# One layout for the four leading expert blocks: seven products first, then their second products, with the Sinkhorn steps at listed points

## The chip, the cores and the metric

The kernel runs on one core of a Trainium2 chip. The metric is the device time of one execution in microseconds (us). Engines are named as in the profile: PE (TensorE), DVE (VectorE), ACT (ScalarE), POOL (GpSimd), SP (the queue that issues DMAs). Each engine runs its instructions in program order, and waits on semaphores where an operand or a buffer is not ready.

## What is computed

Three stages follow one another: a sparse attention (2 batches, 8 heads, 768 tokens, 64 features), a mixture of 8 experts over 1536 tokens of 512 features, and a two-layer network with a rational activation. The change lies in the middle stage:

```python
logits = x @ w_gate                      # 1536 x 8
P = np.exp(logits - logits.max())
for _ in range(8):                       # Sinkhorn steps
    P /= P.sum(1, keepdims=True) + 1e-09
    P /= P.sum(0, keepdims=True) + 1e-09
    P *= N / E
for e in range(E):
    h = np.maximum(x @ w1[e], 0.0)       # 512 -> 1024
    out += P[:, e:e + 1] * (h @ w2[e])   # 1024 -> 512
```

## The kernel before, in words

All matrix products are made of three fp32r matmuls, from operands split into a high and a low part (`hh`, `hl` of a hidden tile, `w2h`, `w2l` of a weight). The order on each engine is the order in which the code is written.

An expert is two units of 512 hidden columns. Unit 0 is done in the plain way, partly under the attention. Units 1 to 15 are cut into halves: sub-units v = 0 to 29, each with 256 hidden columns in two chunks c. Each sub-unit has two blocks, j = 0 and 1, of 768 tokens. A block is written (v, j) here.

- A block makes its hidden layer by a Strassen-like scheme of **seven products** (`product`, six matmuls of 384 columns each) into three PSUM accumulators X, Y and Z (one bank each). DVE and ACT combine them in `s1`, `s2`, `s3`; `hidden(c, half, src)` then makes the relu `hh` on ACT and the rest `hl` on DVE. There are four hidden tiles: two chunks, two halves of the tokens. The last, `hidden(1, 0, X)`, reads the seventh product's X.
- Then come six **second products** (`g2w`, six matmuls of 512 columns each, tile `p_v`): three groups of 128 tokens for each half. DVE adds each to the output sums `accs`. Their PSUM tiles come from a pool of three banks (`psm`); for the later blocks a ring uses two further banks (`psb`) as well.
- In the **later blocks** (v >= VG = 2) the seven products stand in a row (order 0, 2, 1, 4, 3, 6, 5), then three second products held over from the block before (`held`, its half 1), then three of the block's own half 0.
- In the **four leading blocks** (v = 0, 1) the products are in the order 0 to 6, and after each one `step` calls `tick`: it runs a job if one is due, and one second product from the queue `g2q`. So products and second products alternate, and second products run a block after their hidden tiles. The seventh product is added into Y; `hidden(0, 1, s2)` waits in `late` for the next block.
- The **jobs** are the Sinkhorn steps. `sk_max_b` and `sk_max_c` spread the maximum (two small matmuls `mxt`, `mxb`); `sk_first` then normalizes the rows; each `sk_step` is a matmul with ones (`csp`) and nine small DVE operations (four for the columns, L972 to L975, five for the rows, L963 to L967; the last step has only the four). `point` counts calls of `tick`; a job runs at the first point at or after its due number.
- **Weights**: POOL splits the quarters of w1 and their sums (`w_sums`, `w_op`) and w2 (`w2_op`) for the next sub-unit. For v = 0, `w2_op(0, 0)` is written before block (0, 0), into the pool `cv`, and `w2_op(0, 1)` after its seventh product. The conversion of the last stage's weights (`cv_load`, `cv_round`, `cv_join`, `cv_add`, `cv_high`, `cv_low`, `cv_store`) runs beside the blocks from v = 2 on, with a first part in (1, 1).

Three second products of unit 0 are left when block (0, 0) starts; they have twelve matmuls each.

Of the kernel before, what the change touches and what calls it, by code (L numbers as in the profile page):

```python
# [22 lines left out]
def kernel(  # L23
# [1087 lines left out]
    jobs += [(4, sk_max_b), (7, sk_first)]  # L1111
    jobs += [(9 + 2 * i + (i > 1), lambda i=i: sk_step(i == 7)) for i in range(8)]
# [43 lines left out]
    VG = 2  # L1156
    LATER = [0, 2, 1, 4, 3, 6, 5]

    def turn(v, i):
        return LATER[i] if v >= VG else i  # L1160

    def w_op(v, i):
        i = turn(v, i)
# [6 lines left out]
    def w2_op(v, c):  # L1170
        st = sg["v", v, 2]
        pool, tag = (vpool, "cv") if v == c == 0 else (w2pool[1], "w2")
        hi = pool.tile([P, DM], F32R, tag=tag, name=f"w2h_v{v}_{c}")
        lo = pool.tile([P, DM], F32R, tag=tag, name=f"w2l_v{v}_{c}")
        split(hi, lo, st[:, c, :])
        wt["v", v, c] = (hi, lo)

    def sub_weights(v, j, i):

        n = v + 1  # L1180
        if j == 0:
# [25 lines left out]
    late = []  # L1207
# [3 lines left out]
    def step(v):  # L1211
        tick()

    def block(v, j):
# [12 lines left out]
        def product(i, ps, get, start):  # L1227
# [7 lines left out]
            sub_weights(v, j, turn(v, i))  # L1235
# [12 lines left out]

        if v >= VG:
            k = 2 * (v - VG) + j  # L1250
            product(0, X, xs(0, o1), True)
            nc.scalar.copy(s1, X)  # L1252
            if k == 0:
                while late:
                    late.pop()()
                for _ in range(n // P):
                    g2q.pop(0)[1]()
                held[:] = [f for _, f in g2q]
                g2q.clear()
            cv_add(k)  # L1260
            product(2, Z, xs(1, o1), True)
            nc.vector.tensor_add(s1, s1, Z)
            cv_join(k + 1)
# [4 lines left out]
            nc.vector.tensor_add(s2, s2, Y)
            cv_high(k)
            product(3, X, tt(1), False)  # L1270
            nc.scalar.copy(s3, X)
            nc.vector.tensor_add(s3, s3, Y)
            product(6, Z, xs(1, o2), True)
            hidden(1, 1, s3)
# [184 lines left out]
```

## Time and profile before

| what | value |
|---|---|
| median of 3 runs | 1351.94 us (1351.87 to 1351.96) |
| profiled execution | 1352.21 us, span of the trace 1350.5 us |
| PE busy | 1342.1 us (99%) |
| DVE busy | 1052.9 us (78%) |
| POOL busy | 804.3 us (60%) |
| ACT busy | 510.9 us (38%) |

Matmuls are pipelined: the listed duration of one overlaps the next, so PE's pace is read from the starts of its matmuls, not from their durations or from the busy share. DVE's instructions overlap their neighbours by about 0.1 us in the same way.

### The profile page before, as it was taken

The numbers are of one execution on the slowest core, as the hardware profiler recorded it, in microseconds if no ns is written. First come the engines' busy times: TensorE is split into PE (matmuls) and PEld (weight loads), VectorE is DVE, ScalarE is ACT, GpSimd is POOL, SyncE is SP. The second block draws the span as 40 slices with busy tenths as digits, with TensorE's granted clock in tenths as the row PEclk, the third lists the DMA queues.
The fourth block names the chain that finished last, engine by engine and source line by source line (L and its number), as shares of the span: only waits on it lengthen the run. The fifth ranks groups of instructions, "written<-read, shape, count | busy, mean of one in ns | idle before, by whom it ended". The sixth has DMA issues, their size and how long they took to land.

```text
span 1350.5 us, 20263 instructions
## 1 busy us (share of the span) xinstructions
PE 1342.1 (99%) x7343; PEld 1186.0 (88%) x7343; DVE 1052.9 (78%) x1956; ACT 510.9 (38%) x1136; POOL 804.3 (60%) x983
## 2 busy tenths in 40 slices
PE   8999999999999999999999999999999999999999
PEld 6888898999999999999999999999999888888887
DVE  7775588777777777777787777777777689988885
ACT  6874313222222222222222222222222379866662
POOL 7625747777776777776777767777777012222221
PEclk9999999999999999999999999999999999999999
DMA  9730112222222222222222222222222411312102
GB/s 262 169 85 1 51 46 63 89 70 79 67 73 68 67 77 67 83 66 87 69 77 72 67 74 68 76 69 77 75 80 62 146 57 47 94 33 94 32 16 78
DMA packets 122004, 102.40 MB, mean 76 GB/s; under 512 B 36272, under 2 KB 102960, under 8 KB 121904
## 3 DMA queue, kind: packets, MB, share of 16 engines
q1 hardware_dynamic: 121904, 101.10, 25.7%
q8 instruction: 58, 0.95, 0.3%
q14 instruction: 42, 0.34, 0.1%
HBM read 81.15 MB, written 19.92 MB: 75 GB/s over the span
## 4 chain that ended last, share of the span: by engine, by line
PE 97%; DVE 1%; DMA 1%; ACT 0%; SPq 0%; issue 0%; POOL 0%; DVEq 0%; ACTq 0%
PE p_v L185 12%; PE p_v L184 12%; PE p_v L186 12%; PE p L184 8%; PE p L186 8%; PE p L185 8%; PE X L1234 6%; PE X L1232 6%; PE X L1233 6%; PE Z L1233 3%; PE Z L1234 3%; PE Z L1232 3%; PE Y L1234 2%; PE Y L1233 2%; PE Y L1232 2%; PE xo L678 1%
## 5 line engine op out<-in xcount | busy, mean ns | idle before, releaser
L1347 DVE SCALAR_TENSOR_TENSOR accs<-p_v,Pt,accs 128x512 f32<-128x512 f32 x336 | 244.4, 746 | 85.9 <-PE p_v L186 85.2
L184 PE MATMUL p_v<-w2h_v,hh_v 128*128 128x512 f32 x720 | 282.2, 392 | 0.1
L186 PE MATMUL p_v<-w2h_v,hl_v 128*128 128x512 f32 x720 | 281.9, 392 | 0.0
L185 PE MATMUL p_v<-w2l_v,hh_v 128*128 128x512 f32 x720 | 281.7, 391 | 0.0
L1241 DVE SCALAR_TENSOR_TENSOR hl_v<-s,hh_v 128x384 fp32r<-128x384 f32 x180 | 137.4, 763 | 76.0 <-ACT hh_v L1240 74.6
L234 POOL TENSOR_TENSOR hl<-ta,hh 128x512 fp32r<-128x512 f32 x48 | 62.5, 1302 | 204.4 <-ACT hh L233 150.0
L1252 ACT COPY s<-X 128x384 f32<-128x384 f32 x56 | 27.0, 482 | 406.6 <-PE X L1234 406.6
L1041 POOL TENSOR_SCALAR ce<-ce 128x296 uint32<-128x296 uint32 (+1 forms) x56 | 67.1, 1199 | 176.7 <-DVE ce L1032 176.7
L186 PEld LDWEIGHTS p_v<-w2h_v,hl_v 128*128 128x128 f32 x720 | 135.2, 188 | 28.3
L184 PEld LDWEIGHTS p_v<-w2h_v,hh_v 128*128 128x128 f32 x720 | 135.4, 188 | 26.3 <-DVE accs L1342 0.5
L185 PEld LDWEIGHTS p_v<-w2l_v,hh_v 128*128 128x128 f32 x720 | 135.3, 188 | 25.9
L1240 ACT ACTIVATE hh_v<-s 128x384 fp32r<-128x384 f32 x180 | 94.9, 527 | 126.8 <-DVE s L1275 68.6
L110 POOL TENSOR_TENSOR wS<-S,wS 128x256 fp32r<-128x256 f32 x120 | 100.2, 835 | 14.4 <-ACT wS L107 4.7
L184 PE MATMUL p<-xh,w1h 128*128 128x512 f32 (+2 forms) x272 | 100.8, 371 | 0.0
L186 PE MATMUL p<-xh,w1l 128*128 128x512 f32 (+2 forms) x272 | 99.1, 364 | 0.0
L185 PE MATMUL p<-xl,w1h 128*128 128x512 f32 (+2 forms) x272 | 99.1, 364 | 0.0
L184 PE MATMUL p<-w2h,hh 128*128 128x512 f32 (+1 forms) x240 | 94.0, 392 | 0.0
L186 PE MATMUL p<-w2h,hl 128*128 128x512 f32 (+1 forms) x240 | 93.3, 389 | 0.0
L185 PE MATMUL p<-w2l,hh 128*128 128x512 f32 (+1 forms) x240 | 93.2, 388 | 0.0
L110 POOL TENSOR_TENSOR w2l_v<-sb,w2h_v 128x512 fp32r<-128x512 f32 x60 | 82.9, 1382 | 5.0
L1234 PE MATMUL X<-th,wS 128*128 128x384 f32 x240 | 80.3, 335 | 0.0
L1232 PE MATMUL X<-th,wS 128*128 128x384 f32 x240 | 80.3, 335 | 0.0
(249 smaller groups left out, 3309.1 us busy)
## 6 DMA issues: line engine op xcount, KB each, us to landing
sa<-in_moe_w_dram SPq DMA_DIRECT2D x30, 512.0 KB, 3.4
sb<-in_moe_w_dram SPq DMA_DIRECT2D x30, 512.0 KB, 4.3
cv<-in_moe_w_in_dram SPq DMA_DIRECT2D x24, 296.0 KB, 2.9
w1h<-f_in SPq DMA_DIRECT2D x16, 256.0 KB, 2.8
w1l<-f_in SPq DMA_DIRECT2D x16, 256.0 KB, 3.2
w2h<-f_out SPq DMA_DIRECT2D x16, 256.0 KB, 4.9
w2l<-f_out SPq DMA_DIRECT2D x16, 256.0 KB, 5.1
vx<-in_v_dram SPq DMA_DIRECT2D x20, 192.0 KB, 4.2
```

The costliest lines, as they stand in the source:

```text
L110: nc.gpsimd.tensor_sub(lo, src, hi.bitcast(F32))
L184: nc.tensor.matmul(ps, lhsT=sh, rhs=mh, start=(i == 0), stop=False)
L185: nc.tensor.matmul(ps, lhsT=sh, rhs=ml, start=False, stop=False)
L186: nc.tensor.matmul(ps, lhsT=sl, rhs=mh, start=False, stop=(i == n_k - 1))
L234: nc.gpsimd.tensor_sub(hl[:, :n], ta, hh[:, :n].bitcast(F32))
L1041: nc.gpsimd.tensor_scalar(out=e, in0=e, scalar1=896, scalar2=0, op0=ALU.subtract, op1=ALU.max)
L1232: nc.tensor.matmul(ps, lhsT=w[:, 0, t], rhs=mh, start=start and t == 0, stop=False, **go)
L1233: nc.tensor.matmul(ps, lhsT=w[:, 0, t], rhs=ml, start=False, stop=False, **go)
L1234: nc.tensor.matmul(ps, lhsT=w[:, 1, t], rhs=mh, start=False, stop=t == 1, **go)
L1240: nc.scalar.activation(hh, src, AF.Relu)
L1241: nc.vector.scalar_tensor_tensor(out=hl, in0=src, scalar=0.0, in1=hh.bitcast(F32), op0=ALU.max, op1=ALU.subtract)
L1347: nc.vector.scalar_tensor_tensor(out=a, in0=ps, scalar=Pt[:, g, e:e + 1], in1=a, op0=ALU.mult, op1=ALU.add)
```

## The change

The branch for the leading blocks goes. Every block has the layout of the later ones: the seven products in the order 0, 2, 1, 4, 3, 6, 5, the seventh in a bank of its own (Z) with one more DVE addition, then the held second products, then the block's own three. In (0, 0) nothing is held yet; unit 0's three second products stand behind its first product. In the leading blocks a job can run behind the first product, behind the fourth one written (product 4), and behind each second product; the due numbers are given for these points. `w2_op(0, 0)` and `w2_op(0, 1)` are both written behind the second product of (0, 0), in the pool of the other w2 tiles. The conversion's first part follows the later blocks' places. Where the ring of PSUM banks starts (v = 2) is unchanged.

```diff
-    jobs += [(4, sk_max_b), (7, sk_first)]
-    jobs += [(9 + 2 * i + (i > 1), lambda i=i: sk_step(i == 7)) for i in range(8)]
+    jobs += [(1, sk_max_b), (2, sk_first)]
+    jobs += [(due, lambda i=i: sk_step(i == 7)) for i, due in enumerate((4, 7, 9, 12, 15, 18, 21, 23))]
...
             if v == 0:
-                if i == 2:
+                if i == 1:
+                    w2_op(0, 0)
+                    w2_op(0, 1)
+                    dma_sub(1, 2)
+                elif i == 2:
                     w_sums(1)
                 elif 2 < i < 6:
                     w_op(1, i - 3)
-                elif i == 6:
-                    w2_op(0, 1)
-                    dma_sub(1, 2)
...
+    def turn_on():
+        point[0] += 1
+        run_job()
...
+        k = 2 * (v - VC) + j
         product(0, X, xs(0, o1), True)
         nc.scalar.copy(s1, X)
-        while late:
-            late.pop()()
-        step(v)
-        product(1, X, tt(0), False)
-        nc.scalar.copy(s2, X)
-        step(v)
+        if v == j == 0:
+            for _, f in g2q:
+                f()
+            g2q.clear()
+        if v < VC:
+            turn_on()
+        if k >= 0:
+            cv_add(k)
         product(2, Z, xs(1, o1), True)
         nc.vector.tensor_add(s1, s1, Z)
+        if k + 1 >= 0:
+            cv_join(k + 1)
+        product(1, X, tt(0), False)
+        nc.scalar.copy(s2, X)
         hidden(0, 0, s1)
...
+        product(4, Y, xs(0, o2), True)
+        nc.vector.tensor_add(s2, s2, Y)
+        if k >= 0:
+            cv_high(k)
+        else:
+            turn_on()
         product(3, X, tt(1), False)
         nc.scalar.copy(s3, X)
-        step(v)
-        product(4, Y, xs(0, o2), True)
         nc.vector.tensor_add(s3, s3, Y)
+        product(6, Z, xs(1, o2), True)
         hidden(1, 1, s3)
-        step(v)
+        nc.vector.tensor_add(s2, s2, Z)
+        if k >= 0:
+            cv_low(k)
         product(5, X, tt(2), False)
+        hidden(0, 1, s2)
         hidden(1, 0, X)
...
+        for i, f in enumerate(held + seconds_of(0)):
+            f()
+            if i == 0 and k >= 0:
+                cv_store(k)
+            elif i == max(2, len(held)) and k + 2 >= 0:
+                cv_round(k + 2)
+            turn_on()
+        held[:] = seconds_of(1)
```

Two places show the new order. The first is PE at the end of block (0, 0); the product from `wA` into X is the one that `hidden(1, 0, X)` reads. Before:

```order
L1234 MATMUL X_0_2163<-th_1804,wA_0_2155 128x384
L184 MATMUL p_0_8_2268<-w2h_0_746,hh_768_0_1988 128x512
L185 MATMUL p_0_8_2268<-w2l_0_747,hh_768_0_1988 128x512
L186 MATMUL p_0_8_2268<-w2h_0_746,hl_768_0_1989 128x512
L184 MATMUL p_0_8_2268<-w2h_1_750,hh_768_1_2087 128x512
L185 MATMUL p_0_8_2268<-w2l_1_751,hh_768_1_2087 128x512
```

Now:

```order
L1230 MATMUL X_0_2159<-th_1804,wA_0_2154 128x384
L184 MATMUL p_v_0_2310<-w2h_v_0_2224,hh_v_0_00_2247 128x512
L185 MATMUL p_v_0_2310<-w2l_v_0_2225,hh_v_0_00_2247 128x512
L186 MATMUL p_v_0_2310<-w2h_v_0_2224,hl_v_0_00_2248 128x512
L184 MATMUL p_v_0_2310<-w2h_v_1_2228,hh_v_0_10_2306 128x512
L185 MATMUL p_v_0_2310<-w2l_v_1_2229,hh_v_0_10_2306 128x512
L186 MATMUL p_v_0_2310<-w2h_v_1_2228,hl_v_0_10_2307 128x512
```

Behind that product stood a second product of unit 0, whose hidden tiles were old; now the block's own first second product stands there, and its fourth matmul reads `hh_v_0_10`, made from that same X.

The second place is DVE in block (0, 1): a Sinkhorn step between the sums of the products. Before:

```order
L1241 SCALAR_TENSOR_TENSOR hl_v_1_10_2432<-X_1_2295,hh_v_1_10_2431 128x384
L972 TENSOR_SCALAR cr<-csp 128x8
L973 RECIPROCAL cr<-cr 128x8
L974 TENSOR_SCALAR cr<-cr 128x8
L975 TENSOR_TENSOR Pt<-Pt,cr 128x96
L963 TENSOR_REDUCE rs<-Pt 128x12
L964 TENSOR_SCALAR rs<-rs 128x12
L965 RECIPROCAL rr<-rs 128x12
L966 TENSOR_TENSOR Pt<-Pt,rr 128x96
L967 TENSOR_REDUCE cs<-Pt 128x8
L1342 TENSOR_TENSOR accs<-accs,p_v_4_2446 128x512
L1318 TENSOR_TENSOR s_0_1_2299<-s_0_1_2299,Y_1_2296 128x384
```

Now:

```order
L1264 TENSOR_TENSOR s_0_1_2349<-s_0_1_2349,Y_1_2346 128x384
L972 TENSOR_SCALAR cr<-csp 128x8
L973 RECIPROCAL cr<-cr 128x8
L974 TENSOR_SCALAR cr<-cr 128x8
L975 TENSOR_TENSOR Pt<-Pt,cr 128x96
L963 TENSOR_REDUCE rs<-Pt 128x12
L964 TENSOR_SCALAR rs<-rs 128x12
L965 RECIPROCAL rr<-rs 128x12
L966 TENSOR_TENSOR Pt<-Pt,rr 128x96
L967 TENSOR_REDUCE cs<-Pt 128x8
L1271 TENSOR_TENSOR s_0_1_2350<-s_0_1_2350,Y_1_2346 128x384
L1237 SCALAR_TENSOR_TENSOR hl_v_1_11_2433<-s_0_1_2350,hh_v_1_11_2432 128x384
```

The step stood behind the block's `hl_v_1_10`; now it stands ahead of three of the block's four `hl` tiles, and the additions of the second products stand behind all four.

## Rows read from the trace of the kernel before

**Rows 1.** The page: PE's busy time, its granted clock, the chain that ended last.

```profile
PE 1342.1 (99%) x7343; PEld 1186.0 (88%) x7343; DVE 1052.9 (78%) x1956; ACT 510.9 (38%) x1136; POOL 804.3 (60%) x983
...
PEclk9999999999999999999999999999999999999999
...
PE 97%; DVE 1%; DMA 1%; ACT 0%; SPq 0%; issue 0%; POOL 0%; DVEq 0%; ACTq 0%
```

**Rows 2.** Waits of PE, whole span, first of seven: total us, times, longest.

```profile
PE spin L540 <- POOL ident masks.py:199: 1.4, 1, 1.4
```

**Rows 3.** Timeline of PE, first matmul of blocks (0,0) to (3,0): start us, duration us.

```profile
137.84 0.33 PE L1232 MATMUL X<-xh,wA 128*128 128x384 f32 x1
...
153.60 0.33 PE L1232 MATMUL X<-xh,wA 128*128 128x384 f32 x1
...
170.27 0.33 PE L1232 MATMUL X<-xh,wA 128*128 128x384 f32 x1
...
186.67 0.33 PE L1232 MATMUL X<-xh,wA 128*128 128x384 f32 x1
...
203.03 0.34 PE L1232 MATMUL X<-xh,wA 128*128 128x384 f32 x1
...
223.09 0.33 PE L1232 MATMUL X<-xh,wA 128*128 128x384 f32 x1
...
238.60 0.33 PE L1232 MATMUL X<-xh,wA 128*128 128x384 f32 x1
```

**Rows 4.** Timeline of PE around the matmul of one Sinkhorn step.

```profile
161.10 0.28 PE L971 MATMUL csp<-cs,ones 128*128 128x8 f32 x2
161.23 0.48 PE L184 MATMUL p_v<-w2h_v,hh_v 128*128 128x512 f32 x1
161.55 0.39 PE L185 MATMUL p_v<-w2l_v,hh_v 128*128 128x512 f32 x1
```

**Rows 5.** Timeline of all engines at the seventh product's end, block (2,1).

```profile
229.03 0.56 DVE L1272 TENSOR_TENSOR s<-s,Y 128x384 f32<-128x384 f32 x1 [0.56 <-ACT s L1271]
...
230.40 0.39 PE L184 MATMUL p_v<-w2h_v,hh_v 128*128 128x512 f32 x1
...
231.72 0.47 ACT L1240 ACTIVATE hh_v<-X 128x384 fp32r<-128x384 f32 x1
...
232.33 0.55 DVE L1241 SCALAR_TENSOR_TENSOR hl_v<-X,hh_v 128x384 fp32r<-128x384 f32 x1
...
232.84 0.75 DVE L1347 SCALAR_TENSOR_TENSOR accs<-p_v,Pt,accs 128x512 f32<-128x512 f32 x1
```

**Rows 6.** Timeline of DVE, starts and ends of three Sinkhorn steps.

```profile
161.94 0.16 DVE L972 TENSOR_SCALAR cr<-csp 128x8 f32<-128x8 f32 x1
...
164.07 1.16 DVE L966 TENSOR_TENSOR Pt<-Pt,rr 128x96 f32<-128x96 f32 x1
...
165.56 0.68 DVE L1342 TENSOR_TENSOR accs<-accs,p_v 128x512 f32<-128x512 f32 x1
...
169.17 0.15 DVE L972 TENSOR_SCALAR cr<-csp 128x8 f32<-128x8 f32 x1
...
172.24 0.68 DVE L1342 TENSOR_TENSOR accs<-accs,p_v 128x512 f32<-128x512 f32 x1
...
175.11 0.16 DVE L972 TENSOR_SCALAR cr<-csp 128x8 f32<-128x8 f32 x1
...
177.34 0.68 DVE L1342 TENSOR_TENSOR accs<-accs,p_v 128x512 f32<-128x512 f32 x1
```

**Rows 7.** Timeline of POOL under the first two of them.

```profile
163.83 1.28 POOL L110 TENSOR_TENSOR w2l_v<-sb,w2h_v 128x512 fp32r<-128x512 f32 x1
...
167.03 0.74 POOL L1150 TENSOR_TENSOR S<-sa 128x256 f32<-128x256 f32 x1
```

**Rows 8.** Timeline of DVE, start of the maximum's copy, and behind `sk_first`.

```profile
156.47 0.14 DVE L954 COPY nm<-mxb 128x1 f32<-128x1 f32 x1
...
158.36 0.68 DVE L1342 TENSOR_TENSOR accs<-accs,p_v 128x512 f32<-128x512 f32 x1
```

More of the change, by code (lines that the diff above doesn't have):

```diff
@@ L1154, in w_sums @@
         wS[v] = S
[L1156 to L1160, printed above, removed]
+    VC = 2
+    TURN = [0, 2, 1, 4, 3, 6, 5]
     def w_op(v, i):
-        i = turn(v, i)
+        i = TURN[i]
         name = OPS[i]
@@ L1171, in w2_op @@
         st = sg["v", v, 2]
-        pool, tag = (vpool, "cv") if v == c == 0 else (w2pool[1], "w2")
-        hi = pool.tile([P, DM], F32R, tag=tag, name=f"w2h_v{v}_{c}")
-        lo = pool.tile([P, DM], F32R, tag=tag, name=f"w2l_v{v}_{c}")
+        hi, lo = (w2pool[1].tile([P, DM], F32R, tag="w2", name=f"w2{x}_v{v}_{c}") for x in "hl")
         split(hi, lo, st[:, c, :])
@@ L1247, in seconds_of @@
             return [lambda t=t: g2w(v, j, half, t) for t in range(n // P)]
[L1249 to L1253, printed above, removed]
-                while late:
-                    late.pop()()
[L1256 to L1263, printed above, removed]
-            product(1, X, tt(0), False)
-            nc.scalar.copy(s2, X)
-            hidden(0, 0, s1)
-            product(4, Y, xs(0, o2), True)
[L1268 to L1274, printed above, removed]
-            nc.vector.tensor_add(s2, s2, Z)
-            cv_low(k)
-            product(5, X, tt(2), False)
-            hidden(0, 1, s2)
-            hidden(1, 0, X)
-            for i, f in enumerate(held + seconds_of(0)):
-                f()
-                if i == 0:
-                    cv_store(k)
-                elif i == max(2, len(held)):
-                    cv_round(k + 2)
-                point[0] += 1
-                run_job()
-            held[:] = seconds_of(1)
-            return
@@ L1291, in block @@
+        k = 2 * (v - VC) + j
         product(0, X, xs(0, o1), True)
         nc.scalar.copy(s1, X)
-        while late:
-            late.pop()()
-        step(v)
+        if v == j == 0:
[6 more added lines that the diff above has]
+            cv_add(k)
+        product(2, Z, xs(1, o1), True)
+        nc.vector.tensor_add(s1, s1, Z)
+        if k + 1 >= 0:
+            cv_join(k + 1)
         product(1, X, tt(0), False)
@@ L1297, in block @@
         nc.scalar.copy(s2, X)
-        step(v)
-        product(2, Z, xs(1, o1), True)
-        nc.vector.tensor_add(s1, s1, Z)
         hidden(0, 0, s1)
-        first = (v, j) == (VG - 1, 1)
-        if first:
-            cv_round(0)
+        product(4, Y, xs(0, o2), True)
[4 more added lines that the diff above has]
+            turn_on()
         product(3, X, tt(1), False)
         nc.scalar.copy(s3, X)
-        step(v)
-        product(4, Y, xs(0, o2), True)
@@ L1309, in block @@
         nc.vector.tensor_add(s3, s3, Y)
+        product(6, Z, xs(1, o2), True)
         hidden(1, 1, s3)
-        step(v)
+        nc.vector.tensor_add(s2, s2, Z)
+        if k >= 0:
+            cv_low(k)
         product(5, X, tt(2), False)
+        hidden(0, 1, s2)
         hidden(1, 0, X)
-        if first:
-            cv_join(0)
-        step(v)
-        product(6, Y, xs(1, o2), False)
-        nc.vector.tensor_add(s2, s2, Y)
-        late.append(lambda: hidden(0, 1, s2))
-        if first:
-            cv_round(1)
@@ L1322, in block @@
-        for half in range(2):
-            g2q.extend((point[0] + 2, f) for f in seconds_of(half))
-        step(v)
+        for i, f in enumerate(held + seconds_of(0)):
[6 more added lines that the diff above has]
+        held[:] = seconds_of(1)
     def g2w(v, j, half, t):
```

14 lines of the change are left out of this document (5 added, 9 removed).

## The prediction, made before the result was known

> **What bounds the kernel now.** I read the page first. PE is busy 99% of the span, 97% of the chain that ended last is PE, and its clock is granted in full in every slice [rows 1]. So only PE's own pace and its waits count. The list of PE's waits has seven entries, 4.7 us together, the longest 1.4 us, all of them in the attention [rows 2]; among the expert blocks it has none. But the busy share can't show small gaps, because matmuls overlap; so I went on to the starts of the blocks in PE's timeline [rows 3]. A block in the later layout takes 238.60 - 223.09 = 15.51 us. The leading ones (0,1), (1,0) and (1,1) take 16.67, 16.40 and 16.36 us, and hold the same 78 matmuls each, beside Sinkhorn matmuls. That difference is what the change can gain. Then I read DVE, ACT and POOL at the places where the new order has PE wait for them.
>
> **What is removed.** From the start of (0,0) to the start of (2,1) PE now takes 223.09 - 137.84 = 85.25 us. In the new layout without any wait the same work is five blocks of 15.51 us, 77.55 us. (0,0) has unit 0's three second products in the place of three held ones: the six of a later block take 238.60 - 230.40 = 8.20 us [rows 3, 5], 1.37 us each; those of unit 0 have twice the matmuls, so 3 x 1.37 = 4.1 us more. A Sinkhorn matmul takes 0.13 us up to the next start, and the matmul behind it steps 0.32 us instead of 0.23 us [rows 4, 5]: 0.22 us, eight times, 1.8 us. The two matmuls of the maximum have no row; by this nearest one 0.4 us, and 0.8 us if dear; I take 0.6 us. Sum 77.55 + 4.1 + 1.8 + 0.6 = 84.05 us. So the row layout **gives back 1.2 us** (1.0 to 1.4), the price of going to and fro between 384 and 512 columns and of the small gap that the late hidden tile costs.
>
> **What stands against it: (0,0).** Nothing is held over, so right behind the seventh product PE wants, after three matmuls (3 x 0.23 = 0.69 us), the hidden tile of chunk 1 that is made from this very product. In (2,1) that tile's `hh` ends 231.72 + 0.47 - 230.40 = 1.79 us after the seventh product, its `hl` 232.33 + 0.55 - 230.40 = 2.48 us after [rows 5]; there 4.1 us of held products hide it. Here PE waits 1.79 - 0.69 = 1.1 us for `hh`, then does two matmuls (0.46 us, at 2.25), then waits 0.23 us for `hl`: 1.3 us. Besides, `sk_first` now stands on DVE ahead of `s3`. It takes 158.36 - 156.47 = 1.89 us from the copy of the maximum to its end [rows 8], with ACT's exponential inside. DVE gets to that copy about 1.1 us after product 4 (sum into s2 behind `hl_00`, two operations of about 0.5 us), so it ends 3.0 us after product 4. From product 4 to the end of the seventh are three products, 3 x 1.04 (7.31 us for seven, 223.09 to 230.40) and 0.5 us of the maximum's matmul, 3.6 us; s3's sum starts 230.40 - 229.03 = 1.37 us ahead of that end when nothing is in its way [rows 5], so at 2.2 us. The delay is 0.8 us. If DVE is slowed by POOL, which is at the sums and splits of sub-unit 1 then, it is up to 1.7 us. Wait in (0,0): 2.1 to 3.1 us, **I take 2.5**.
>
> **(0,1).** After product 4 DVE does its sum and then a whole Sinkhorn step, then s3 and the rest. A step takes 177.34 - 175.11 = 2.23 us where POOL is idle, 172.24 - 169.17 = 3.07 us and 165.56 - 161.94 = 3.62 us where POOL splits weights [rows 6, 7]. With 1.1 us ahead of it, s3 starts 3.3 to 4.7 us after product 4. From s3's start to the first addition are 232.84 - 229.03 = 3.81 us [rows 5], and the addition takes 0.68 us [rows 6]; so the first PSUM bank comes free 7.8 to 9.2 us after product 4. The leading blocks have three banks for second products. PE gets to the fourth after three products, three held ones and two Sinkhorn matmuls, 3.12 + 4.1 + 0.44 = 7.7 us. Wait: 0.1 to 1.5 us. Then the next step (due 9) starts two additions later on DVE, and its column sums are wanted by the matmul (due 12) two second products on, 2.75 us: started 0.6 us after the bank came free it ends at 2.8 to 3.7 us (2.23 and 3.07 us), 0.1 to 0.9 us late. The sixth second product needs the bank of the third, whose addition stands behind that step, 0.68 us more, less the small matmul: 0.5 us. Sum 0.7 to 2.9 us. POOL is in this block at four splits behind products, w2's two tiles and the next sums, one after the other, as it is under the first two steps of [rows 6]; so I take the side of these rows, **2.2 us**.
>
> A step's dear operation there is L966, 1.16 us while POOL's `w2l` runs (from 163.83, 1.28 us) [rows 6, 7]. The Trainium skill (SBUF — State Buffer, Who interferes with whom) says that a DVE instruction with two SBUF inputs and a GpSimd one that reads SBUF take one read interface by turns, each for the whole instruction, and that reductions are exempt. The rows agree. By that rule the places given to the steps in (0,1) are poor ones, and the sum stays at the contended end; without it, 1.5 us less.
>
> **(1,0) and (1,1).** In (1,0) POOL has run ahead and is idle, so a step is 2.23 us and PE's wait for the fourth bank is 0.1 us. In (1,1) the last step has four of nine operations, an estimated 1 us of the 2.23, but the conversion's join (two operations on DVE, by its neighbours' 0.5 us each some 1 us) and POOL's splits come in: 0 to 1.4 us (what the slow steps of [rows 6] lost), **I take 0.5**.
>
> **Moved at no cost.** w2 of sub-unit 0: two tiles, each a copy and a rest, the rest 1.28 us [rows 7], some 2 us a tile. They wait for the tiles of unit 0, which the third second product of unit 0 gives free from some 2 us before its end on, and so are done about 2.2 us after it; PE wants them six products (6.2 us) and one small matmul later. Cover left: some 4 us; if it were gone, PE would wait for the excess alone. Behind them on POOL the sums of sub-unit 1 start some 5 us later than now; they are wanted in (1,0), 30 us on. SP's loads of w2 for sub-unit 1 and of the conversion come earlier, since the tiles they wait for are free earlier. One more DVE addition in each leading block is in the 3.81 us above, as (2,1) has it. After (1,1) all is as now.
>
> **Sum.** -1.2 + 2.5 + 2.2 + 0.1 + 0.5 = **+4.1 us**. The profiled execution took 1352.21 us (span 1350.5 us and 1.7 us around it), 0.27 us over the median; its new time would be 1356.3 us, and the median 1351.94 + 4.1 = 1356.0 us. Ends: -1.4 + 2.1 + 0.7 + 0 + 0 = +1.4 (1353.3 us), and -1.0 + 3.1 + 2.9 + 0.3 + 1.4 = +6.7 (1358.6 us).
>
> **Rivals.** (A) The forecast: DVE's in-order queue ends the waits, 1356.0 us. (B) The same waits, but the steps in (0,1) run at 2.23 us as in the third of [rows 6], and (0,0) and (1,1) stay at their low ends: -1.2 + 2.1 + 0.7 + 0.1 = +1.7 us, 1353.6 us, no difference that counts. It decides if POOL's splits fall beside the steps instead of on them, a matter of a microsecond. For it speaks that the third step of [rows 6] ran free while the two ahead of it did not, so that little decides; against it that POOL in (0,1) has no free time. (C) The other side: DVE and ACT keep up so that PE waits nowhere, and the 1.2 us remain, 1350.7 us. For it speaks that no later block has a wait; it needs the last hidden tile within 0.7 us of its product in (0,0), where (2,1) shows 1.8 us, which speaks against it. (D) The waits add up: each late addition moves the next step, and (0,1) and (1,1) pay the whole step each time; two more steps, 2 x 2.2 us over A, 1360.4 us. Against it: the products of each block, 7.3 us, let DVE catch up.
>
> **How the numbers follow.** 0.2% of the time, about what a measurement of this kernel can tell from no change, is 2.7 us. Chances: A 0.65, B 0.27, C 0.05, D 0.03. A and D are slower by more than that, 0.68; B lies within, and so does C's 1.2 us, 0.30 with 0.02 left for a C that gains more than 2.7 us by a way that no row here shows, 0.02. The range holds B and A with their bounds: 1353.2 to 1358.6 us.
>
> **What would show it.** In the changed profile the list of PE's waits should name the first `p_v` of (0,0), held up by ACT's `hh_v` and then DVE's `hl_v` (2.5 us), and `p_v` and `csp` in (0,1) held up by DVE's `accs` and `cs` (2.2 us). (0,0) should take about 22.9 us, (0,1) about 18.4 us, (1,0) about 16.3 us, (1,1) about 16.2 us, (2,0) 15.5 us, against 15.76, 16.67, 16.40, 16.36 and 20.06 us now [rows 3]. Wrong would be: a first `p_v` that doesn't wait; Sinkhorn steps on DVE in (0,1) under 2.5 us; or a change after (2,1), which this sum doesn't know.

## The result, and the profile after

The changed kernel takes 1359.32 us (median of 6 runs, 1358.71 to 1360.25), the kernel before 1351.95 us (6 runs, 1351.82 to 1352.03): **7.4 us slower**, a ratio of 1.0055 with an interval of 1.0042 to 1.0068. Slower was forecast with the highest chance; but the time lies 3.3 us over the forecast of 1356.0 us and 0.7 us over the upper end of the range.

The page of after, as in [rows 1]: PE is busy for a little longer, and in the chain that ended last it gives a point to DVE and ACT.

```profile
PE 1343.7 (99%) x7343; PEld 1185.1 (87%) x7343; DVE 1053.7 (78%) x1960; ACT 511.7 (38%) x1136; POOL 805.5 (59%) x983
...
PE 96%; DVE 2%; ACT 1%; DMA 1%; issue 0%; SPq 0%; POOL 0%; ACTq 0%; DVEq 0%
```

The list of PE's waits in after (total us, times, longest us). In [rows 2] the spin matmul of the attention led it; now two waits in the expert blocks do, and `csp` is in it as well:

```profile
PE p_v L184 <- DVE accs L1305: 2.5, 3, 2.0
PE p_v L184 <- ACT hh_v L1236: 2.3, 1, 2.3
PE spin L540 <- POOL ident masks.py:199: 1.4, 1, 1.4
...
PE csp L971 <- DVE cs L967: 0.5, 1, 0.5
```

PE's timeline of after, first matmul of blocks (0,0) to (2,1) (start us, duration us), to be held against [rows 3]:

```profile
137.41 0.33 PE L1228 MATMUL X<-xh,wA 128*128 128x384 f32 x1
...
162.23 0.33 PE L1228 MATMUL X<-xh,wA 128*128 128x384 f32 x1
...
181.90 0.33 PE L1228 MATMUL X<-xh,wA 128*128 128x384 f32 x1
...
198.26 0.42 PE L1228 MATMUL X<-xh,wA 128*128 128x384 f32 x1
...
214.64 0.33 PE L1228 MATMUL X<-xh,wA 128*128 128x384 f32 x1
...
230.14 0.33 PE L1228 MATMUL X<-xh,wA 128*128 128x384 f32 x1
```

From the first to the last of them are 92.73 us, against 85.25 us before: 7.48 us more. What comes behind is as long as it was (1357.6 - 230.14 = 1127.5 us, and 1350.5 - 223.09 = 1127.4 us). So the whole loss lies in the five blocks, (0,0) and (0,1) above all. Differences of such starts, in us (taken before rounding, so the last digit can differ by one from the lines shown):

| kernel | (0,0) | (0,1) | (1,0) | (1,1) | (2,0) | sum |
|---|---|---|---|---|---|---|
| before | 15.76 | 16.67 | 16.40 | 16.35 | 20.06 | 85.25 |
| predicted | 22.9 | 18.4 | 16.3 | 16.2 | 15.5 | 89.3 |
| after | 24.81 | 19.67 | 16.36 | 16.38 | 15.51 | 92.73 |

**(0,0).** PE's timeline of after behind the seventh product:

```profile
153.54 0.39 PE L184 MATMUL p_v<-w2h_v,hh_v 128*128 128x512 f32 x1
...
154.00 0.40 PE L186 MATMUL p_v<-w2h_v,hl_v 128*128 128x512 f32 x1
156.75 0.47 PE L184 MATMUL p_v<-w2h_v,hh_v 128*128 128x512 f32 x1 [2.35 <-ACT hh_v L1236]
...
158.47 0.63 PE L184 MATMUL p_v<-w2h_v,hh_v 128*128 128x512 f32 x1
158.89 0.63 PE L185 MATMUL p_v<-w2l_v,hh_v 128*128 128x512 f32 x1
159.32 0.63 PE L186 MATMUL p_v<-w2h_v,hl_v 128*128 128x512 f32 x1
```

The wait is the forecast one: the fourth matmul starts 156.75 - 154.00 - 0.23 = 2.5 us late and its releaser is the last hidden tile on ACT. What nobody had forecast stands below it. From 158.47 on the matmuls start 0.43 us apart instead of 0.23 us. The view by stretches says why (width of the stretch; PE, PEld, DVE, ACT and POOL busy with counts; granted clock; DMA):

```profile
155.00:158.00 3.00, 1.25 (x5) 0.88 (x6) 1.76 (x5) 0.90 (x2) 0.73 (x1) 1.00 0.00 0
158.00:160.00 2.00, 2.00 (x8) 1.57 (x7) 0.58 (x2) 0.00 (x0) 0.00 (x0) 0.56 0.00 0
160.00:162.00 2.00, 2.00 (x6) 1.64 (x7) 1.81 (x7) 0.00 (x0) 0.00 (x0) 0.59 0.00 0
```

The granted clock, which was 1.00 in these blocks before, falls to its lower level (1.2 instead of 2.4 GHz) soon after the wait, for some 3.4 us (158.2 to 161.6 us), and costs about 1.6 us. PE counts as fully busy in that time, and the 40 slices of the page's clock line don't show it.

**(0,1).** DVE's timeline of after, from the first hidden tile to the first additions:

```profile
166.51 1.10 DVE L1237 SCALAR_TENSOR_TENSOR hl_v<-s,hh_v 128x384 fp32r<-128x384 f32 x1 [1.35 <-ACT hh_v L1236]
...
168.00 0.15 DVE L972 TENSOR_SCALAR cr<-csp 128x8 f32<-128x8 f32 x1
...
169.43 0.25 DVE L963 TENSOR_REDUCE rs<-Pt 128x12 f32<-128x96 f32 x1
169.71 0.97 DVE L964 TENSOR_SCALAR rs<-rs 128x12 f32<-128x12 f32 x1
...
171.66 0.54 DVE L1271 TENSOR_TENSOR s<-s,Y 128x384 f32<-128x384 f32 x1
...
175.56 1.27 DVE L1305 TENSOR_TENSOR accs<-accs,p_v 128x512 f32<-128x512 f32 x2
```

One of POOL's two longest splits of that block lies under L964, the fourth of these lines:

```profile
169.37 1.28 POOL L110 TENSOR_TENSOR w2l_v<-sb,w2h_v 128x512 fp32r<-128x512 f32 x1
```

And PE, which waits for the additions and for the sums:

```profile
173.90 0.40 PE L186 MATMUL p_v<-w2h_v,hl_v 128*128 128x512 f32 x1
176.28 0.50 PE L184 MATMUL p_v<-w2h_v,hh_v 128*128 128x512 f32 x1 [1.99 <-DVE accs L1305]
...
178.92 0.39 PE L186 MATMUL p_v<-w2h_v,hl_v 128*128 128x512 f32 x1
179.82 0.39 PE L971 MATMUL csp<-cs,ones 128*128 128x8 f32 x2 [0.52 <-DVE cs L967]
180.41 0.50 PE L184 MATMUL p_v<-w2h_v,hh_v 128*128 128x512 f32 x1 [0.20 <-DVE accs L1305]
```

The three waits are those that were forecast, in their order and with their releasers: the bank of the fourth second product, the column sums, the bank of the sixth. But the first is 2.0 us in the list and 176.28 - 173.90 - 0.23 = 2.15 us by the starts, instead of 0.1 to 1.5 us. The other two are 179.82 - 178.92 - 0.23 = 0.67 us and 180.41 - 179.82 - 0.13 = 0.46 us by the starts, within what was forecast (0.1 to 0.9 us, and 0.5 us). The Sinkhorn step takes 171.66 - 168.00 = 3.66 us, and the hidden tile ahead of it 1.10 us.

### The profile page after: what moved, and what is told of

Its sections match the earlier page's. It is cut to its first block, busy times and chain, and to the rows that moved or that the text cites. A ratio compares the mean times of both kernels' runs of the same rounds, so it can differ in the third digit from the quotient of the medians.

```text
span 1357.6 us, 20265 instructions
## 1 busy us (share of the span) xinstructions
PE 1343.7 (99%) x7343; PEld 1185.1 (87%) x7343; DVE 1053.7 (78%) x1960; ACT 511.7 (38%) x1136; POOL 805.5 (59%) x983
## 4 chain that ended last, share of the span: by engine, by line
PE 96%; DVE 2%; ACT 1%; DMA 1%; issue 0%; SPq 0%; POOL 0%; ACTq 0%; DVEq 0%
PE p_v L186 12%; PE p_v L184 12%; PE p_v L185 12%; PE p L184 8%; PE p L186 8%; PE p L185 8%; PE X L1228 6%; PE X L1230 6%; PE X L1229 6%; PE Z L1228 3%; PE Z L1230 3%; PE Z L1229 3%; PE Y L1228 1%; PE Y L1230 1%; PE Y L1229 1%; PE xo L678 1%
## 5 line engine op out<-in xcount | busy, mean ns | idle before, releaser
L184 PE MATMUL p_v<-w2h_v,hh_v 128*128 128x512 f32 x720 | 282.2, 392 | 4.9 <-DVE accs L1305 2.5
L186 PE MATMUL p_v<-w2h_v,hl_v 128*128 128x512 f32 x720 | 282.2, 392 | 0.0
L185 PE MATMUL p_v<-w2l_v,hh_v 128*128 128x512 f32 x720 | 281.7, 391 | 0.0
L184 PEld LDWEIGHTS p_v<-w2h_v,hh_v 128*128 128x128 f32 x720 | 135.5, 188 | 32.6 <-DVE accs L1305 3.4
L186 PEld LDWEIGHTS p_v<-w2h_v,hl_v 128*128 128x128 f32 x720 | 135.4, 188 | 28.7 <-DVE hl_v L1237 0.3
L185 PEld LDWEIGHTS p_v<-w2l_v,hh_v 128*128 128x128 f32 x720 | 135.5, 188 | 26.6
L184 PE MATMUL p<-xh,w1h 128*128 128x512 f32 (+2 forms) x272 | 100.7, 370 | 0.0
L186 PE MATMUL p<-xh,w1l 128*128 128x512 f32 (+2 forms) x272 | 99.0, 364 | 0.0
L185 PE MATMUL p<-xl,w1h 128*128 128x512 f32 (+2 forms) x272 | 99.0, 364 | 0.0
L184 PE MATMUL p<-w2h,hh 128*128 128x512 f32 (+1 forms) x240 | 93.7, 390 | 0.0
L186 PE MATMUL p<-w2h,hl 128*128 128x512 f32 (+1 forms) x240 | 93.2, 388 | 0.0
L185 PE MATMUL p<-w2l,hh 128*128 128x512 f32 (+1 forms) x240 | 93.0, 388 | 0.0
L1228 PE MATMUL X<-th,wS 128*128 128x384 f32 x240 | 80.5, 336 | 0.0
L1229 PE MATMUL X<-tl,wS 128*128 128x384 f32 x240 | 80.2, 334 | 0.0
```

The source lines that it names most:

```text
L184: nc.tensor.matmul(ps, lhsT=sh, rhs=mh, start=(i == 0), stop=False)
L185: nc.tensor.matmul(ps, lhsT=sh, rhs=ml, start=False, stop=False)
L186: nc.tensor.matmul(ps, lhsT=sl, rhs=mh, start=False, stop=(i == n_k - 1))
L1228: nc.tensor.matmul(ps, lhsT=w[:, 0, t], rhs=mh, start=start and t == 0, stop=False, **go)
L1229: nc.tensor.matmul(ps, lhsT=w[:, 0, t], rhs=ml, start=False, stop=False, **go)
```

## The experiments

The theory: the row layout itself gains a little, and all that is lost are PE's waits in (0,0) and (0,1), with the stretch at the lower clock behind one of them. Times are compared with runs of the kernel before on the same chip (1351.8 to 1351.9 us each time).

### The wait in (0,0) covered

The three second products of unit 0 are held back behind the seventh product, as the later blocks do with theirs; w2 then needs other places, two hidden tiles too, and the due numbers move up by three points.

```diff
                 if i == 1:
                     w2_op(0, 0)
-                    w2_op(0, 1)
-                    dma_sub(1, 2)
...
-            for _, f in g2q:
-                f()
+            held[:] = [f for _, f in g2q]
             g2q.clear()
...
+            if v == j == 0 and i == 2:
+                w2_op(0, 1)
+                dma_sub(1, 2)
```

> The changed kernel, but unit 0's three second products stand behind the seventh product of (0,0), as held ones do in the other blocks, and not behind the first. To make room, two hidden tiles of (0,0) lie in buffers that the sums of x no longer use, w2 of sub-unit 0's first chunk is made early in the conversion's buffer, the second chunk behind the three, and the due numbers after (0,0) are three higher. Theory (queues and clock): the 2.7 us wait for the last hidden tile of (0,0) is covered, and with it the 3.4 us of half clock behind it, worth 1.7 us, do not come: 1359.3 - 4.4 = 1354.9 us, and runs scatter by under 0.3 us. Rival (DVE's load): DVE cannot keep up whatever stands there and the wait moves to the block's own second products or to (0,1): 1357.5 us or more.

Measured: 1355.45 us (1354.82 to 1355.82), ratio 1.0026 (1.0016 to 1.0036). (0,0) takes 20.82 us, and of its wait nothing is left. The list of PE's waits of this kernel begins with (0,1):

```profile
PE p_v L184 <- DVE accs L1310: 2.1, 1, 2.1
```

The lower clock is still there, now behind that wait (view by stretches of this kernel):

```profile
173.00:175.00 2.00, 2.00 (x7) 1.60 (x6) 1.80 (x6) 0.00 (x0) 1.92 (x4) 0.58 0.00 0
```

So the expectation that the lower clock would not come was wrong: covering the wait in (0,0) takes 4.0 us off that block, wait and stretch together, and the stretch then follows the next long wait. There it costs less: (0,1) takes 20.18 us, 0.5 us more than the 19.67 us of after at full clock, because PE, being slower, no longer waits for `csp` behind it. (1,1) is 0.5 us shorter, as in the run with two fillers below. The kernel gains 3.9 us in all.

### Other due numbers, one point apart

```diff
-(4, 7, 9, 12, 15, 18, 21, 23)
+(4, 6, 9, 11, 14, 17, 19, 22)
```

> The changed kernel, but no Sinkhorn step stands behind product 4, that is between the sums of the products; they run behind the first product of a block or behind second products (due 4, 6, 9, 11, 14, 17, 19, 22). Theory: the waits of (0,1) come of the step ahead of s3's sum, 3.7 us on DVE; without it the fourth second product no longer waits 2.2 us, the steps between the second products still cost about 1 us: 1359.3 - 2.2 = 1357.1 us. Rival (DVE's load): the step costs the same wherever it stands in the block, 1359 us within 0.5. Wait and half clock in (0,0) stay with both.

Measured: 1357.81 us (1357.00 to 1359.55), ratio 1.0045 (1.0030 to 1.0060). `s3` is no longer late in (0,1), and the wait for the bank is gone (0.2 us left). In its place `csp` waits for DVE's `cs`, 2.1 us in two times, since the step behind the second product is started by DVE only when it has made the late hidden tiles and two additions (173.98 us), and the next `csp` stands two second products on. (0,1) is hardly shorter, 19.38 us. In the profiled execution no stretch at the lower clock lies in these blocks, and (0,0) takes 23.25 us, 1.56 us less than in after with the same wait: that is the price of the stretch. That the median comes near the expected 1357.1 us is partly luck: the expectation kept the stretch, and two of the four executions (1357.00 and 1357.02 us) have a mean clock of 1.000, while (0,1) lost 0.3 us and not 2.2 us. So this run speaks as much for its rival: moving the steps exchanges one wait for another unless they are also far enough apart.

### Five PSUM banks for the leading blocks

```diff
-        if v >= VC:
-            ring[0] += 1
+        ring[0] += 1
```

> The changed kernel, but the ring of five PSUM banks for second products starts with sub-unit 0 and not with sub-unit 2. Theory: the fourth second product of (0,1) no longer waits for a bank (until 176.3 us), only for its hidden tile, which DVE ended at 175.6 us: 0.7 to 1.3 us less, 1358.3 us, with the waits of csp about as they are. Rival (banks): three banks are the whole cause in (0,1), and all of its waits go, 3.2 us: 1356.1 us.

Measured: 1361.32 us (1359.85 to 1361.53), ratio 1.0070 (1.0053 to 1.0087), 2 us slower than after; both expectations failed. (The profiled execution, with one stretch at the lower clock as in after's, takes 1359.85 us, 0.6 us more than after's; the three others have a mean clock of 0.997.) PE's timeline of this kernel in (0,1):

```profile
178.31 0.39 PE L971 MATMUL csp<-cs,ones 128*128 128x8 f32 x2 [1.89 <-DVE cs L967]
180.10 0.80 PE L184 MATMUL p_v<-w2h_v,hh_v 128*128 128x512 f32 x1 [1.40 <-DVE accs L1304]
```

The fourth and fifth second product hardly wait any more, so PE gets to `csp` 1.3 us sooner after the block's start, and waits there, and for the bank behind it again. `csp` takes its tile from the two banks that the ring now uses as well. More banks don't help when DVE is what is late.

### Matmuls without a use in the place of the wait

Nine matmuls of 512 columns into an unused tile ahead of the second products of (0,0), which PE does while it would wait.

```diff
+        if v == j == 0:
+            fill = psb.tile([P, 512], F32, tag="g", name="fill")
+            for i in range(9):
+                nc.tensor.matmul(fill, lhsT=th[0][:, 0, 0:P], rhs=xh[:, 2, 0:512], start=True, stop=True)
```

> The changed kernel with nine further matmuls (128x512, 2.1 us, into a spare bank that nobody reads) between the seventh product of (0,0) and the block's first second product, so that PE has work while ACT and DVE make the hidden tile. Theory (the wait makes the clock fall): the wait's end is unchanged, the clock stays at 2.4 GHz, 1359.3 - 1.7 = 1357.6 us, and the runs agree within 0.3 us. Rival (the clock falls for another reason): the half clock behind it stays and the scatter of 1.5 us stays, 1359.3 us.

Measured: 1357.77 us (1357.12 to 1358.16), ratio 1.0043 (1.0028 to 1.0058), 1.6 us less than after although nothing is ready earlier. (0,0) takes 23.25 us at full clock. The runs did spread, which was not expected, and in the profiled one, the slowest, the lower clock was back behind the wait in (0,1), where it makes the block 0.4 us longer (20.16 us against 19.75 us in the next run). The next run does away with both.

> After with matmuls into an unused tile in the place of PE's two long waits: nine of 512 columns ahead of the second products in (0,0), and nine ahead of the fourth second product in (0,1), about 2.1 us each. No result is made earlier, so PE's useful work starts no sooner; only the engine isn't idle meanwhile. Theory (the half clock follows from the idle time): no half-clock stretch ahead of the end, blocks 23.2, 18.5, 16.4, 15.8 and 15.5 us, +4.2 us over before, 1356.1 us. Rival (the half clock, if any, costs nothing beyond the waits): 1357.8 us, as with the first of the two fillers alone.

```diff
+            if v == 0 and j == 1 and i == 3:
+                fill = psb.tile([P, 512], F32, tag="g", name="fill")
+                for _ in range(9):
+                    nc.tensor.matmul(fill, lhsT=th[0][:, 0, 0:P], rhs=xh[:, 2, 0:512], start=True, stop=True)
```

Measured: 1357.41 us (1357.22 to 1357.74), ratio 1.0041 (1.0026 to 1.0057). All four executions have a mean granted clock of 1.000; the view by stretches of this kernel shows it where after had 0.56:

```profile
158.00:160.00 2.00, 2.00 (x12) 1.67 (x11) 1.31 (x3) 0.00 (x0) 0.00 (x0) 1.00 0.00 0
```

The time is 1.9 us below after. By the block times 1.56 us of that lie in (0,0), which is the clock's price. Another 0.5 us lie in (1,1), 15.88 instead of 16.38 us, and are not the clock's: there a hidden tile met POOL's split of w2 in after and made PE wait for a bank, and it didn't here, where POOL's copy beside it took 1.03 us instead of 0.62 us. DVE's timeline, after first, then this kernel:

```profile
208.28 1.03 DVE L1237 SCALAR_TENSOR_TENSOR hl_v<-s,hh_v 128x384 fp32r<-128x384 f32 x1 [0.65 <-ACT hh_v L1236]
```

```profile
206.76 0.56 DVE L1237 SCALAR_TENSOR_TENSOR hl_v<-s,hh_v 128x384 fp32r<-128x384 f32 x1 [0.65 <-ACT hh_v L1236]
```

The figure of 1356.1 us was too low because it had 18.5 us for (0,1), which takes 19.67 us in after at full clock; with 19.75 us measured, the five blocks are 90.75 us, +5.5 us, as timed. The waits by themselves, less the layout's gain, cost 7.48 - 1.56 = **5.9 us of the 7.5 us** in the trace of after.

### A wait put into the kernel before

```diff
+            if (v, j) in ((3, 1), (5, 1), (6, 1)):
+                gate.append(ht["v", v, j, 1, 0][1])
...
+        if gate:
+            nc.tensor.matmul(ps[:, 0:P], lhsT=gate[0][:, 0:P], rhs=gate.pop()[:, 0:P], start=True, stop=True)
         mm3(ps, 2, get)
```

> The kernel before, with one more small matmul (128 columns, its result written over at once) ahead of the first held second product in (3,1), (5,1) and (6,1), which reads the low part of the last hidden tile; so PE waits there for DVE as it does in (0,0) of after, some 2.5 us each time, in blocks that are otherwise undisturbed. Theory (a wait of this length is followed by a stretch at half clock that costs 1.7 us): 3 x (2.5 + 0.1 + 1.7) = 12.9 us, 1364.8 us. Rival (a wait costs its own length): 3 x 2.6 = 7.8 us, 1359.7 us. If the half clock follows only some of the waits, the time lies between and the runs spread.

Measured: 1361.64 us (1360.00 to 1361.69), ratio 1.0069 (1.0055 to 1.0083). It lies between the two: one stretch at the lower clock for three waits. PE's timeline of this kernel at the three waits:

```profile
263.76 0.33 PE L1343 MATMUL p_v<-hl_v 128*128 128x128 f32 x1 [2.37 <-DVE hl_v L1242]
...
328.56 0.47 PE L1343 MATMUL p_v<-hl_v 128*128 128x128 f32 x1 [2.38 <-DVE hl_v L1242]
...
329.36 0.63 PE L185 MATMUL p_v<-w2l_v,hh_v 128*128 128x512 f32 x1
329.79 0.63 PE L186 MATMUL p_v<-w2h_v,hl_v 128*128 128x512 f32 x1
...
363.72 0.33 PE L1343 MATMUL p_v<-hl_v 128*128 128x128 f32 x1 [2.37 <-DVE hl_v L1242]
```

The stretch comes with the second wait. The first and the third, as long, bring none; the matmuls behind them start 0.23 to 0.28 us apart. Of the four executions one has a mean clock of 1.000 and takes 1360.00 us, the others 1361.64 to 1361.69 us at 0.998 to 0.999 (the trace is one of these). So a wait costs (1360.00 - 1351.86) / 3 = 2.7 us, its own length with the small matmul, and a stretch 1.6 us more when it comes. A wait of 2.4 us can bring it in a kernel that never has it otherwise; it doesn't always.

### The steps moved to where DVE has time

In after, with nothing else changed, the first step stays behind the second own product of (0,0), the next one goes behind the first product of (0,1), and the others behind the third or the last second product of a block; none stands between product 4 and the late hidden tiles.

```diff
-(4, 7, 9, 12, 15, 18, 21, 23)
+(4, 6, 10, 13, 18, 21, 26, 29)
```

> After with the steps moved alone, behind the third or the last second product of a block or the first product; the wait in (0,0) stays. Theory: (0,0) 23.2 us and 1.7 us of half clock behind its wait, the others 16.0, 16.0, 16.0 and 15.5 us, 88.4 us in all, +3.2 us over before, 1355.1 us; no wait for accs in (0,1). Rival (the wait in (0,1) comes from the late last hidden tile, as that in (0,0), and not from the steps): (0,1) still waits about 2 us and the time stays over 1357.5 us.

Measured: 1355.98 us (1354.45 to 1356.16), ratio 1.0027 (1.0018 to 1.0037). (0,1) takes 17.22 us instead of 19.67 us, with 0.3 us of wait each for `accs` and `cs`; (1,0) and (1,1) take 15.97 us each. The wait in (0,0) is as in after. So in (0,1) most of the loss goes with the place of the steps. The nine executions fall into two groups: 1354.45 and 1354.53 us at a mean clock of 1.000, and seven from 1355.60 to 1356.16 us at 0.999, 1.5 us apart. The same program, the same wait; by time and mean clock the stretch follows it in seven cases of nine. The trace is of the first group and has none.

### Both waits gone

The first experiment's cover, with the steps near these places: each step behind the third or the last second product of a block, with nothing between product 4 and the late hidden tiles (the points are numbered with three more in (0,0); the line taken out is the first experiment's).

```diff
-(7, 10, 12, 15, 18, 21, 24, 26)
+(5, 8, 13, 16, 21, 24, 29, 32)
```

> The layout of after with unit 0's three second products held back behind the seventh product of (0,0), and the eight Sinkhorn steps moved so that each stands behind the third or the last second product of a block, none between product 4 and the late hidden tiles. Theory (all that is lost are PE's waits in (0,0) and (0,1) and the half clock behind one of them; the row layout itself gives 1.2 us back): PE waits nowhere in these blocks, they take 20.8, 16.0, 16.0, 16.0 and 15.5 us, 84.3 us against 85.25 us before, no half-clock stretch ahead of the end, and the time is 1351.0 us (1350.5 to 1351.5), below the kernel before. Rival (the steps hold DVE up wherever they stand, because POOL splits weights in these blocks): a wait of 1 us or more remains in (0,1) or (1,0), and the time is 1353.5 us or more.

Measured: 1351.18 us (11 runs; ten of them 1350.98 to 1351.32, one 1352.44), against 1351.86 us before (20 runs, 1351.74 to 1352.58). The ratio is 0.9995 (0.9987 to 1.0004). The blocks take 21.00, 16.02, 15.98, 15.97 and 15.57 us, 84.54 us, with the rest as before. The list of PE's waits of this kernel begins as [rows 2] does:

```profile
PE spin L540 <- POOL ident masks.py:199: 1.4, 1, 1.4
```

The list names no wait in these blocks and the clock is full, as the theory has it. One small gap is left in (0,0), ahead of the seventh product, which goes into X: ACT still copies X until 144.56 us, since that copy stands behind the exponential of `sk_first` (ACT and PE, this kernel):

```profile
143.81 0.38 ACT L955 ACTIVATE Pt<-Pt,nm 128x96 f32<-128x96 f32 x1 [1.92 <-DVE nm L954]
144.10 0.46 ACT L1272 COPY s<-X 128x384 f32<-128x384 f32 x1
```

```profile
144.27 0.34 PE L1229 MATMUL Z<-xh,wS 128*128 128x384 f32 x1
144.61 0.45 PE L1227 MATMUL X<-th,wA 128*128 128x384 f32 x1
```

The two starts are 0.34 us apart and the next one 0.28 us behind, instead of 0.17 us each: 0.27 us. The first experiment's kernel has the same gap; after doesn't have it (152.33 and 152.50 us, 0.17 us apart). As it stands, this kernel gains 0.7 us in the trace and in the medians; the interval of the ratio doesn't exclude no change.

### POOL kept off DVE in (0,1)

POOL's weight splits of (0,1) are held back behind a POOL copy of one column of the first accumulator that the block updates. The steps stand where after has them.

```diff
-            sub_weights(v, j, TURN[i])
+            if (v, j) == (0, 1):
+                later.append(TURN[i])
+            else:
+                sub_weights(v, j, TURN[i])
...
+            if later:
+                nc.gpsimd.tensor_copy(zz, acc[HB // P][:, 0:1])
+                for t in later:
+                    sub_weights(v, j, t)
+                later.clear()
```

> After with POOL kept off DVE in the first part of (0,1): the splits of sub-unit 1's weights that POOL makes there (eight of w1, four of w2) are held back behind a one-column POOL copy of the accumulator that the first second product of (0,1) has updated, so POOL starts them some 9 us later, behind the hidden tiles; they are wanted in (1,0) only. The Sinkhorn steps stand where they stand in after. Theory (the step between product 4 and s3 makes PE wait because POOL's splits stretch DVE's operations): the low part of the first hidden tile takes 0.55 instead of 1.10 us, the step 2.2 instead of 3.66 us, so PE's wait for the fourth PSUM bank in (0,1) falls from 2.0 us to under 0.3 us, (0,1) takes 17.6 us, and the time falls by 2 us, to about 1357.3 us; the wait in (0,0) stays and so does the half clock in most runs. Rival (DVE's queue is too long there in any case): the wait stays over 1.2 us and the time is 1358.5 us or more.

Measured: 1374.34 us (1372.88 to 1374.47), ratio 1.0163 (1.0146 to 1.0180). (0,1) takes 17.63 us, as the theory says to the tenth; but (1,0) takes 20.19 us, and each block behind (2,1) 15.73 instead of 15.51 us, which no theory here knew. The new tile `zz` of 4 bytes was the suspect, so the copy was sent into a tile that exists already.

> As the run with POOL's splits held back in (0,1), but the one-column copy goes into a tile that is there already, so that no tile of SBUF lies at another address than in after. Theory (the 11.9 us that were lost there behind (2,1), evenly in all blocks, came from the new 4-byte tile, which moved the tiles laid out behind it; the contention moved from (0,1) to (1,0) with the splits): the blocks behind (2,1) take 15.51 us again, (0,1) takes 17.6 us, (1,0) some 18.5 to 20.2 us as there, and the time is about 1362 us (1360 to 1363). Rival (the later splits themselves slow PE down to the end): blocks of 15.73 us and about 1374 us again.

```diff
-                nc.gpsimd.tensor_copy(zz, acc[HB // P][:, 0:1])
+                nc.gpsimd.tensor_copy(sk["mx"], acc[HB // P][:, 0:1])
```

Measured: 1360.05 us (1359.22 to 1361.86), ratio 1.0062 (1.0047 to 1.0077); the later blocks take 15.51 us again. DVE's timeline of this kernel in (0,1), to be held against the same lines of after above:

```profile
166.71 0.56 DVE L1241 SCALAR_TENSOR_TENSOR hl_v<-s,hh_v 128x384 fp32r<-128x384 f32 x1 [1.35 <-ACT hh_v L1240]
...
167.64 0.16 DVE L972 TENSOR_SCALAR cr<-csp 128x8 f32<-128x8 f32 x1
...
168.58 0.25 DVE L963 TENSOR_REDUCE rs<-Pt 128x12 f32<-128x96 f32 x1
168.87 0.17 DVE L964 TENSOR_SCALAR rs<-rs 128x12 f32<-128x12 f32 x1
...
169.89 0.55 DVE L1275 TENSOR_TENSOR s<-s,Y 128x384 f32<-128x384 f32 x1
```

With POOL idle the step takes 169.89 - 167.64 = 2.25 us instead of 3.66 us, the hidden tile 0.56 instead of 1.10 us; `s3` starts 1.97 us sooner behind that tile's start (3.18 against 5.15 us), which is the 2.0 us of the bank's wait. (0,1) falls by 2.06 us to 17.61 us. Some 1.4 us over the block without waits (16.02 us and one `csp` more, 0.2 us) stay, with the steps where they are. But the splits now lie on the steps of (1,0), and PE waits there (its timeline, this kernel):

```profile
194.39 0.47 PE L184 MATMUL p_v<-w2h_v,hh_v 128*128 128x512 f32 x1 [2.04 <-DVE accs L1314]
```

The contention has moved by a block, and a second stretch at the lower clock follows that wait in the profiled execution (0.50 from 197 to 199 us).

### One unused tile more

In the kernel without waits, ahead of the other tiles on its side of SBUF: one element, 4 bytes, in the first run, and 12 elements, 48 bytes, in the second.

```diff
+    pad = cpool.tile([P, 1], F32, name="pad")
+    nc.gpsimd.memset(pad, 0.0)
```

> The layout with the three products held back and the steps moved (1351.2 us), with one unused tile of 4 bytes more in the pool of constants, ahead of the other tiles on that side of SBUF. Theory (the place of the tiles alone costs PE): blocks of 15.73 instead of 15.51 us, second products at 234 instead of 227 ns a matmul, 1351.2 + 12 = 1363 us. Rival: 1351.2 us, as without the tile.

> The same with 48 bytes instead of 4, so that the tiles behind start at another offset, one that is a multiple of 16 bytes from the present one. Theory (the offset matters, not that there is one tile more): blocks of 15.5 us and 1351.2 us, or less if the present place isn't the best. Rival (any tile more costs it): 1363 us.

Measured: 1364.33 us (1364.23 to 1364.67), ratio 1.0092 (1.0076 to 1.0109), with 4 bytes, and 1354.41 us (1354.26 to 1354.61), ratio 1.0019 (1.0009 to 1.0028), with 48. One group of the second products between 300 and 1100 us in the kernel without the tile, with 4 bytes and with 48 (busy us, mean ns):

```profile
L186 PE MATMUL p_v<-w2h_v,hl_v 128*128 128x512 f32 x606 | 236.9, 391 | 0.0
```

```profile
L186 PE MATMUL p_v<-w2h_v,hl_v 128*128 128x512 f32 x609 | 240.7, 395 | 0.0
```

```profile
L186 PE MATMUL p_v<-w2h_v,hl_v 128*128 128x512 f32 x607 | 239.1, 394 | 0.0
```

There is no wait in these blocks in either; matmuls are a little longer, with 4 bytes those of all three lines (L184, L185, L186), with 48 bytes those of L186 above all, while L184 keeps its 390 ns. By the starts a later block takes 15.73 and 15.56 us instead of 15.51 us. The 13.2 us and 3.2 us come from where the tiles lie, and the loss depends on the offset; that 48 bytes would cost nothing was wrong. Which operand it is stays open. In all other kernels here but the first with POOL held back, a later block takes 15.51 us, so the comparisons above are not disturbed by it.

## Why the prediction was right in sign and too low

Point by point, in us; what was measured is taken from differences between block times of the runs above:

| step of the prediction | predicted | measured | from |
|---|---|---|---|
| the row layout without waits | -1.2 | -0.7 | no waits: 84.54 - 85.25 |
| wait in (0,0) | 2.5 (2.1 to 3.1) | 2.4 | 23.25 - 20.82, full clock less covered |
| waits in (0,1) | 2.2 (0.7 to 2.9) | 3.4 | 19.67 - 16.02, less a `csp` of 0.2 |
| waits in (1,0) and (1,1) | 0.6 | 0.8 | 32.73 - 31.95, as many `csp` |
| the lower clock | not in the sum | 1.6 | 24.81 - 23.25 |
| sum | +4.1 | +7.5 | trace: +7.48 |

**What held.** The bound (PE's pace and waits) and the mechanism of the likeliest case, DVE's in-order queue: the list of waits names the lines and releasers that were forecast, and the step placed between product 4 and `s3` is what makes (0,1) wait (steps moved: -2.45 us). The wait in (0,0) was right to 0.2 us; w2 was made from 144.6 to 148.6 us, long before its use, at no cost; behind (2,1) nothing changed. Rival C, no wait at all, did not come; its price of 1350.7 us can be held against the layout with both waits taken away, 1351.2 us.

**What failed first: a term that wasn't in the sum.** The prediction read from [rows 1] that the clock is granted in full, concluded that only PE's own pace and its waits count, and kept the full pace behind the waits that it added. But the full clock is that of a kernel in which PE doesn't wait in these blocks. A forecast of a 2.5 us wait needed the question what the clock does after it: the trace of after shows it at 0.56 and 0.59 there, and with the gap filled at 1.00. With 1.6 us for it the forecast would have been 1357.6 us.

**What failed second: the size of the waits in (0,1),** by 1.2 us, 0.5 us over the upper end. Only the first of the three waits, that for the bank of the fourth second product, is out of its bounds. The step was to be 2.23 to 3.62 us by [rows 6] and took 3.66 us; its end of the range was right and was not taken as the likeliest. And the contention was charged to the step alone: the hidden tile ahead of it, put at some 0.5 us among the "1.1 us ahead of it", took 1.10 us under the same POOL work. With these two the first addition comes where the trace has it. The run with POOL held back shows what the contention is worth: 2.06 us of (0,1) go with POOL's splits. The run with the steps moved takes 2.45 us off the same block with POOL as it was; so the two together make the loss, and either one taken away leaves 1.0 to 1.4 us of it. The rule that the prediction drew from the Trainium skill (SBUF — State Buffer, Who interferes with whom) bears this out: the page names two-input operations and operations like `tensor_scalar` in their faster modes as those that can contend with GpSimd, and reductions as exempt. Here L964, a `TENSOR_SCALAR` of 12 elements, takes 0.97 us with POOL at work and 0.17 us without, the hidden tile 1.10 and 0.56 us, the reduction L963 0.25 us in both.

**What failed third: the layout's own gain,** 0.7 instead of 1.2 us. It had been summed from blocks of 15.51 us; in the run without waits the blocks with two Sinkhorn matmuls take 15.97 to 16.02 us, nearly as summed (15.51 + 2 x 0.22 = 15.95), but (0,0) takes 21.00 us, where its parts give 15.51 + 4.1 + 2 x 0.22 + 0.6 = 20.65 us. Of this difference 0.27 us are the gap ahead of the seventh product in the two kernels that hold unit 0's products back, and not a cost of the layout: in after, which doesn't have this gap, the layout gains some 1.0 us, the low end of its range, and the wait in (0,0) costs some 2.7 us instead of 2.4 us (2.5 us ahead of the fourth matmul, and 0.2 us in slower steps behind it). The sum stays as it is.

**What stays open.** After which waits the clock falls: it came with the second of three equal waits, by time and mean clock in seven of nine executions of one program, and in no trace with a filled wait. That is enough to show that the waits bring it and what it costs, 1.6 us where PE has no other wait behind it and 0.4 to 0.5 us in (0,1), but not for a forecast of when.

## What to carry to other kernels

A wait of some 2 us on a PE that is otherwise never idle can cost its own length and up to 1.6 us more; when a sum makes a bound engine wait, ask what its clock does next, and price a run with useless matmuls in the gap before believing the wait alone. When a layout moves a chain of small operations on an in-order engine, place each link behind the work that others wait for, and far enough from the next link; here that, with the first wait covered by work held back, turned +7.4 us into -0.7 us (the latter with an interval that doesn't exclude no change). Contention can be moved out of one block and come up in the next: read the neighbour's waits before calling it solved.

## What the runs showed of the hardware that was not expected

- The granted clock fell to half for some 3.4 us around the end of waits of 1.9 to 2.4 us or soon behind it, and matmuls of 512 columns then started 0.43 us apart instead of 0.23 us. It did so in most executions and not in all, which made the executions of one program differ by 1.5 to 1.6 us in two programs.
- Useless matmuls in the gap of (0,0) kept the clock at 1.00 there and made the block 1.56 us shorter, though nothing was ready earlier.
- An unused tile of 4 bytes among the constants cost 13.2 us in a kernel without any wait, one of 48 bytes 3.2 us: a later block took 15.73 and 15.56 us instead of 15.51 us, all along.
